# A fused attention and two FFN layers on one core: the first phase issued in the order of its source

## The chip, the cores and the metric

The kernel runs on one core of a Trainium2 chip. The core has a matrix engine (TensorE, PE in the rows), a vector engine (VectorE, DVE), a scalar engine (ScalarE, ACT), GpSimd (POOL) and a queue that issues DMAs (SyncE, SP). Each engine works off its own list of instructions in order; semaphores join the lists. The metric is the time of one execution on the device in microseconds; the kernel before is given by three such runs and by one further execution under the hardware profiler.

## The reference

Attention over 4 batches, 8 heads, 768 positions and 64 features with a local window of 96 and 8 global columns, then two FFN layers of 3072 tokens, 512 wide, 2048 hidden. The FFN weights arrive as 64-bit floats.

```python
scores = scale * np.matmul(q, k.transpose(0, 1, 3, 2))
is_global = pos[None, :] < int(n_global)
is_local = (rel >= 0) & (rel < int(n_local))
scores = scores + bias[None, :, :, :]
scores = np.where(is_global | is_local, scores, -1000000000.0)
a = np.exp(scores - np.max(scores, axis=-1, keepdims=True))
a = a / (np.sum(a, axis=-1, keepdims=True) + 1e-09)
x = np.matmul(a, v)          # then to [tokens, 512]
h = x @ w_in;  x = (h - np.tanh(h)) @ w_out      # first layer
h = x @ w_in2; x = (h * np.cos(h)) @ w_out2      # second layer
```

## The kernel before

**Passes.** Each FFN layer's 16 hidden slices of 128 are cut in two halves of NH = 8, so there are four passes P = 0 to 3. Pass 0 (first half of the first layer) runs during the attention, in blocks of N1 = 256 tokens; passes 1 to 3 follow in blocks of 512 tokens. A block step is ("in", P, j, f): twelve matmuls into h (`ffn_in`), then tanh on ScalarE, a subtraction t and a cast g on VectorE and a remainder on GpSimd; or ("out", P, j, f): twelve matmuls from g into the accumulators c (`ffn_out`). An out step comes two steps of f after its in step. Matmuls run with every operand split into a rounded part and its remainder, three products a matmul.

**Units.** The attention has 24 tiles of 128 tokens and two groups of four heads: 48 units, n = 0 to 47, with tile i = n // 2 and group g = n % 2. Block j of pass 0 needs x of tiles 2j and 2j + 1, so it may begin when unit 4j + 3 is through. A unit has these pieces:
- `load_qk`, `load_v`: DMAs on SP. `qk_T`: four transpositions of q and k into PSUM (tp). `qk_hi` (ScalarE) and `qk_lo` (VectorE) copy them out, split.
- `att_s`: twelve score matmuls into s; then for each of four heads a reduction on VectorE (mask, row extreme, e) and an exponential on ScalarE. After the change the second half is `att_e`, in two parts z = 0, 1.
- `att_n`: sums, reciprocals and four scalings of e on VectorE. `att_t`, z = 0, 1: transpositions of e into tp (one PSUM buffer, shared with `qk_T` outside the early units) and the copy pt on ScalarE.
- `att_v`: matmuls with v into x; then for g = 1 the copies xt, the rounded part on ScalarE and the remainder on VectorE. After the change these copies are `att_x`.

Units are pipelined: in `quad(n)` stand the scores of unit n, the transpositions of unit n - 1 and the values of unit n - 2, with four calls of `ffn_step` between them. The first units (`early_quad`, 0 to 3) have no FFN; `busy` puts idle matmuls there.

**Weights.** Each 128 x 512 weight slice is loaded raw (512 KB) and passes four stages, `w_stage(0..3)`: split (ScalarE copy and GpSimd subtraction), join (two VectorE passes), scale and tail (one ScalarE pass each). `w_step` does all four. Pass 0 needs 16 slices at the start; `w_load_far` puts raw slices in the room of later weights, the rest goes through two raw buffers.

**Order.** A scheduler sets each engine's list when the kernel is built. The kernel before pins part of it: `in_turn` issues a piece after the last matmul of the piece before, and `later` issues weight stages after a marked activation and vector instruction. What is not pinned goes where the scheduler puts it.

## Time and profile before

| what | value |
|---|---|
| median of 3 runs | 1312.69 us (1308.87 to 1313.41) |
| profiled execution, its own time | 1309.77 us |
| its span, first to last instruction | 1308.0 us |
| TensorE busy | 1257.8 us, 96% |
| VectorE busy | 777.2 us, 59% |
| ScalarE busy | 567.8 us, 43% |
| GpSimd busy | 389.8 us, 30% |
| mean granted TensorE clock | 0.986 of full |

Busy shares are averages over stretches of different kinds: the first 100 us hold the early units and the turning of 16 weights, up to 480 us attention and pass 0 run together, the rest is passes 1 to 3. Stretches are therefore read apart. The span leaves out 1.8 us of the execution's own time.

### The profile page before, as it was taken

The page shows a single profiled execution, that of the slowest core. Times are in us where ns is not written, and L with a number is a line of the kernel's source. Part 1 is how long each engine was busy: PE and PEld are TensorE (multiplying, and loading weights), DVE is VectorE, ACT ScalarE, POOL GpSimd, SP SyncE. Part 2 cuts the span into 40 slices and gives each one's busy share as a digit, 9 for nine tenths or more (in the row PEclk, how much of TensorE's full clock was granted, in tenths as well). Part 3 has the DMA queues.
Part 4 walks back from the last instruction along what each step waited for, and adds up shares of the span by engine and source line. Part 5 has one row for each costly group of instructions (what it writes and reads, how often), then busy time and mean ns, then how long its engine had stood idle before and what let it go on. Part 6 is the DMA issues. An engine that isn't in the chain of part 4 may idle for free.

```text
span 1308.0 us, 20613 instructions
## 1 busy us (share of the span) xinstructions
PE 1257.8 (96%) x7616; PEld 1074.2 (82%) x7618; DVE 777.2 (59%) x1813; ACT 567.8 (43%) x1287; POOL 389.8 (30%) x343
## 2 busy tenths in 40 slices
PE   7689999999999999999999999999999999999997
PEld 4578988999998998888888888888888888888885
DVE  7786666667676642344433457777765466555563
ACT  6765555565655531223322334554343333333331
POOL 1341221222222223445544533333332122222221
PEclk9689999999999999999999999999999999999999
DMA  9243334433343343344634432333211312332110
GB/s 274 82 126 100 106 109 124 121 100 95 110 130 108 101 156 104 122 152 161 209 124 153 174 129 81 124 102 127 83 57 72 129 65 68 126 111 83 65 65 35
DMA packets 160845, 149.28 MB, mean 114 GB/s; under 512 B 84960, under 2 KB 119776, under 8 KB 160736
## 3 DMA queue, kind: packets, MB, share of 16 engines
q1 hardware_dynamic: 160448, 147.88, 35.8%
q8 instruction: 62, 1.02, 0.3%
q14 instruction: 47, 0.39, 0.1%
q10 hardware_dynamic: 288, 0.00, 0.0%
HBM read 103.81 MB, written 44.04 MB: 113 GB/s over the span
## 4 chain that ended last, share of the span: by engine, by line
PE 90%; DVE 5%; ACT 3%; issue 1%; DMA 0%; POOL 0%; DVEq 0%; POOLq 0%; ACTq 0%; SPq 0%
PE h L429 41%; PE o L466 20%; PE o L460 10%; PE c L460 10%; PE tp L364 3%; PE s L326 3%; PE x L381 2%; ACT e L342 1%; DVE e L339 1%; PE tp L284 1%; PE tp L286 1%; DVE xt L393 1%; DVE wf L70 1%; DVE e L354 1%; DVE wf L67 0%
## 5 line engine op out<-in xcount | busy, mean ns | idle before, releaser
L445 POOL TENSOR_TENSOR g<-t,g 128x512 fp32r<-128x512 f32 (+1 forms) x240 | 267.7, 1116 | 733.5 <-DVE g L444 647.1
L429 PE MATMUL h<-x,wi 128*128 128x512 f32 x1728 | 423.4, 394 | 0.0
L429 PEld LDWEIGHTS h<-x,wi 128*128 128x128 f32 x1728 | 324.1, 188 | 75.9
L466 PE MATMUL o<-wo,g 128*128 128x512 f32 x1152 | 275.5, 390 | 0.0
L466 PEld LDWEIGHTS o<-wo,g 128*128 128x128 f32 x1152 | 216.3, 188 | 47.1
L429 PE MATMUL h<-xt,wi 128*128 128x256 f32 x1152 | 168.0, 294 | 14.8 <-ACT xt L392 11.1
L438 ACT ACTIVATE t<-h 128x256 f32<-128x256 f32 (+1 forms) x144 | 65.2, 454 | 263.6 <-PE h L429 259.3
L439 DVE TENSOR_TENSOR t<-h,t 128x256 f32<-128x256 f32 (+1 forms) x144 | 73.4, 510 | 171.4 <-ACT t L438 170.5
L429 PEld LDWEIGHTS h<-xt,wi 128*128 128x128 f32 x1152 | 147.4, 194 | 25.3 <-ACT xt L392 13.7
L460 PE MATMUL c<-g,wo 128*128 128x256 f32 x1152 | 161.4, 289 | 0.0
L460 PEld LDWEIGHTS c<-g,wo 128*128 128x128 f32 x1152 | 145.2, 192 | 0.2
L414 ACT ACTIVATE t<-t 128x512 f32<-128x512 f32 x96 | 60.6, 631 | 191.9 <-DVE t L413 191.7
L460 PE MATMUL o<-g,wo 128*128 128x512 f32 x576 | 139.1, 390 | 0.0
L460 PEld LDWEIGHTS o<-g,wo 128*128 128x128 f32 x576 | 108.1, 188 | 23.8
L416 DVE SCALAR_TENSOR_TENSOR t<-t,h 128x512 f32<-128x512 f32 x96 | 65.8, 686 | 101.8 <-ACT t L415 101.6
L342 ACT ACTIVATE e<-e,nmall 128x256 f32<-128x256 f32 (+1 forms) x192 | 92.6, 487 | 76.2 <-DVE nmall L339 76.2
L444 DVE CAST g<-t 128x512 fp32r<-128x512 f32 (+1 forms) x240 | 100.8, 421 | 26.2 <-DMA yd<-g 9.2
L339 DVE CUSTOM_DVE_ANT_0 e<-s,M 128x256 f32<-128x256 f32 (+1 forms) x192 | 69.1, 397 | 68.3 <-PE tp L364 57.6
L411 DVE SCALAR_TENSOR_TENSOR t<-ki,h 128x512 f32<-128x512 int32 x96 | 65.7, 685 | 68.5 <-ACT ki L410 68.3
L410 ACT ACTIVATE ki<-h 128x512 int32<-128x512 f32 x96 | 56.9, 595 | 108.9 <-PE h L429 108.6
L412 DVE SCALAR_TENSOR_TENSOR t<-ki,t 128x512 f32<-128x512 int32 x96 | 87.2, 908 | 2.8
L80 POOL TENSOR_TENSOR wi<-wf,wi 128x512 fp32r<-128x512 f32 x32 | 43.6, 1362 | 92.3 <-ACT wi L79 82.3
(83 smaller groups left out, 1176.8 us busy)
## 6 DMA issues: line engine op xcount, KB each, us to landing
x<-yd SPq DMA_DIRECT2D x48, 512.0 KB, 5.7
raw<-in_moe_w_out_dram SPq DMA_DIRECT2D x28, 512.0 KB, 3.6
raw<-in_moe_w_in_dram SPq DMA_DIRECT2D x27, 512.0 KB, 3.8
xd<-xt SPq DMA_DIRECT2D x12, 1024.0 KB, 5.2
x<-xd SPq DMA_DIRECT2D x24, 512.0 KB, 6.3
yd<-g SPq DMA_DIRECT2D x24, 512.0 KB, 4.0
qn<-in_q_dram SPq DMA_DIRECT2D x48, 128.0 KB, 2.4
kn<-in_k_dram SPq DMA_DIRECT2D x48, 128.0 KB, 2.8
```

The costliest lines, as they stand in the source:

```text
L339: mark[1] = nc.vector.tensor_tensor_reduce(out=e[:, j, 0:n], in0=s[j][:, z, 0:n], in1=M[:, z, m0:m0 + n], scale=slopes[4 * g + j] / base, ...
L342: mark[0] = nc.scalar.activation(out=e[:, j, 0:n], in_=e[:, j, 0:n], func=AF.Exp, scale=-1.0, bias=nmall[:, col:col + 1], accum_out=sm[:, ...
L411: mark[1] = nc.vector.scalar_tensor_tensor(out=r, in0=ki, scalar=-C1, in1=h, op0=ALU.mult, op1=ALU.add)
L412: nc.vector.scalar_tensor_tensor(out=r, in0=ki, scalar=-C2, in1=r, op0=ALU.mult, op1=ALU.add)
L416: nc.vector.scalar_tensor_tensor(out=r, in0=r, scalar=-0.5, in1=h, op0=ALU.add, op1=ALU.mult)
L429: m = nc.tensor.matmul(h, lhsT=wk[:, a], rhs=x[:, b], start=(n == 0), stop=(n == 3 * KC - 1))
L438: mark[0] = nc.scalar.activation(out=t, in_=h, func=AF.Tanh)
L439: mark[1] = nc.vector.tensor_tensor(out=t, in0=h, in1=t, op=ALU.subtract)
L444: nc.vector.tensor_copy(out=g[:, 0], in_=t)
L445: nc.gpsimd.tensor_tensor(out=g[:, 1], in0=t, in1=g[:, 0].bitcast(F32), op=ALU.subtract)
L460: m = nc.tensor.matmul(o[z], lhsT=w[:, a, z * 128:(z + 1) * 128], rhs=g[:, b], start=(f == 0 and n == 0 and (P > 0 or z % 2 == 0)), stop=( ...
L466: nc.tensor.matmul(o[z], lhsT=g[:, a, z * 128:(z + 1) * 128], rhs=w[:, b], start=(f == 0 and n == 0), stop=(last and n == 2))
```

## The change

`in_turn` and `later` go. From the first load to the end of attention (`whole`), `in_order` makes every instruction of an engine follow the one before it in the source, on all five engines, so the order of the source is the order of the lists. The source of that phase is rewritten: score matmuls of the early units stand one unit ahead, in a second PSUM buffer (`att_s(*at(n + 1), ...)` in `early_quad(n)`), there are five early units instead of four, `e` of early units lives in the weight pool, weight stages are written one by one between the pieces (`w_stage`, `w_more`), three far loads are asked for per early unit until the 16 slices are asked for, idle matmuls are 5 + 5 x 8 instead of 9 + 4 x 6, and six empty block steps become two. In the first two steps of a block, the out step of the block before stands ahead of the in step, and where x completes a block (`n % 4 == 1`) `att_x` stands ahead of the exponentials.

```diff
+@contextmanager
+def in_order(tc):
+
+    block = tc.nc.cur_bb
+    done = block.bb.instructions
+    first = done[-1] if done else None
+    yield
+    assert tc.nc.cur_bb is block
+    n = next((k for k in reversed(range(len(done))) if done[k] is first), -1) + 1
+    last = {}
+    for i in done[n:]:
+        if i.engine in last:
+            tc.add_manual_dep(
+                i, last[i.engine].name,
+                mybir.DependencyInfo(mybir.DependencyClass.NoSync, mybir.DependencyReason.DATA), reason="in_order")
+        last[i.engine] = i
+
...
+        Sb[i, g] = (s, sm, n, m0)
+
+    Eb = {}
+
+    def att_e(i, g, z, pool=None):
+
+        s, sm, n, m0 = Sb[i, g]
+        if pool is None:
             e = pa.tile([128, 2, 256], F32, tag="e", name="e", bufs=3)
...
+        else:
+            e = pool.tile([128, 2, 256], F32, tag=("wi", "wo")[z], name="e", bufs=16)
+        for j in range(2):
+            col = i * H + 4 * g + 2 * z + j
+            nc.vector.tensor_tensor_reduce(
+                out=e[:, j, 0:n], in0=s[j][:, z, 0:n], in1=M[:, z, m0:m0 + n], scale=slopes[4 * g + j] / base,
+                scalar=BIG, op0=ALU.add, op1=ALU.min, accum_out=nmall[:, col:col + 1])
+            nc.scalar.activation(
+                out=e[:, j, 0:n], in_=e[:, j, 0:n], func=AF.Exp, scale=-1.0,
+                bias=nmall[:, col:col + 1], accum_out=sm[:, 2 * z + j:2 * z + j + 1])
+        Eb[i, g, z] = e
...
+    def att_x(i, g):
+
+        b, t = where(i)
+        x = Xb[i]
         if g == 1:
...
+    strict = [True]
+    whole = ExitStack()
+    whole.enter_context(in_order(tc))
+    nc.vector.memset(zero, 0.0)
     load_qk(0, 0)
     load_qk(0, 1)
-    nc.vector.memset(zero, 0.0)
...
-    busy(9)
-    with in_turn():
-        qk_T(0, 0)
+    busy(5)
+    qk_T(0, 0)
+    qk_T(0, 1, ps_c, "c0")
     qk_hi(0, 0)
     qk_lo(0, 0)
+    qk_hi(0, 1)
     setup_bias()
-    with in_turn():
-        qk_T(0, 1, ps_c, "c0")
-    qk_hi(0, 1)
-    qk_lo(0, 1)
+    att_s(0, 0)
...
-    def next_qk(n, pool=None, tag="tp"):
+    def next_T(n, pool=None, tag="tp"):
 
         i, g = at(n)
         if i + 1 < NTILE:
             qk_T(i + 1, g, pool, tag)
+        if i + 2 < NTILE:
+            load_qk(i + 2, g)
+        if g == 1 and 0 < i < NTILE - 1:
+            load_v(i + 1)
+
+    def next_qk(n):
+        i, g = at(n)
+        if i + 1 < NTILE:
             qk_hi(i + 1, g)
             qk_lo(i + 1, g)
-        if i + 2 < NTILE:
...
     def early_quad(n):
 
         cur, old, old2 = at(n), at(n - 1), at(n - 2)
-        if old in Sb:
+        for z in range(2):
+            att_e(*cur, z, w_pool)
+        if n == 0:
+            qk_lo(0, 1)
+        if n < 4:
+            att_s(*at(n + 1), None if n % 2 else ps_h)
+        next_T(n, ps_c, "c0")
+        busy(4)
+        if old:
             att_n(*old)
-        with in_turn():
-            att_s(*cur, ps_h if n % 2 else None)
+            att_t(*old, 0)
+        w_stage(1)
+        next_qk(n)
         if n == 0:
-            with later():
-                setup_before()
-        with in_turn():
-            busy(3)
-        with in_turn():
-            next_qk(n, ps_c, "c0")
-        next_v(n)
+            setup_before()
+        if old2:
+            att_v(*old2)
+            att_x(*old2)
         if old:
-            with in_turn():
-                att_t(*old, 0)
-            with in_turn():
-                att_t(*old, 1)
-        with in_turn():
-            busy(3)
-        if old2:
-            with in_turn():
-                att_v(*old2)
-        with later():
-            for _ in range((0, 1, 1, 2)[n]):
-                w_step()
-        for _ in range(2):
-            w_load_far()
+            att_t(*old, 1)
+        busy(4)
+        w_stage(0)
+        w_stage(2)
+        w_stage(3)
+        for _ in range(3):
+            if nload[0] < 2 * NH:
+                w_load_far()
...
         if old in Sb:
             att_n(*old)
         if cur:
-            with in_turn():
-                att_s(*cur)
+            att_s(*cur)
         if old2:
-            with in_turn():
-                att_v(*old2)
+            att_v(*old2)
+        if old2 and n % 4 == 1:
+            att_x(*old2)
+        if cur:
+            att_e(*cur, 0)
+        if old2 and n % 4 != 1:
+            att_x(*old2)
         ffn_step()
         if old:
-            with in_turn():
-                att_t(*old, 0)
+            att_t(*old, 0)
+        if cur:
+            att_e(*cur, 1)
+        w_more(0, 1)
         ffn_step()
         if old:
-            with in_turn():
-                att_t(*old, 1)
+            att_t(*old, 1)
+        if cur:
+            att_n(*cur)
+        w_more(2, 3, 0, 1)
         ffn_step()
         if cur:
-            with in_turn():
-                next_qk(n)
-            next_v(n)
+            next_T(n)
+            next_qk(n)
+        w_more(2, 3, 0, 1)
         ffn_step()
-        if cur:
-            att_n(*cur)
-
-    seq = [None] * 6
+        w_more(2, 3)
+        if n == 5:
+            w_more(0, 1, 2, 3)
+
+    seq = [None]
     for P in range(4):
         steps = [(P, j, f) for j in range(NB[P]) for f in range(NH)]
         done = 0
         for n in range(len(steps) + LAG[P]):
-            if n < len(steps):
-                seq.append(("in",) + steps[n])
-
+
+
+            due = []
             while done < len(steps) and (
                     done <= n - LAG[P] or (P > 0 and done == n - LAG[P] + 1 and steps[done][2] == NH - 1)):
-                seq.append(("out",) + steps[done])
+                due.append(("out",) + steps[done])
                 done += 1
+            now = [("in",) + steps[n]] if n < len(steps) else []
+            if P == 0 and n < 2:
+                seq += now + [None] * (n == 0)
+            elif P == 0 and n % NH < 2:
+                seq += due + now
+            else:
+                seq += now + due
     seq.reverse()
 
-    strict = [True]
-
     def ffn_step():
-        if strict[0]:
-            with in_turn():
-                ffn_part()
-        else:
-            ffn_part()
-
-    def ffn_part():
         step = seq.pop()
         if step is None:
-            with later():
-                w_step()
             return
...
-        if P == 0 and j == 0 and nsplit[0] < 2 * NH:
-            with later():
-                w_step()
-
-        if kind == "out" and P < 3:
-            first = NH if P == 0 else 0
-            share = (j * NH + f - 3 - first) / (NB[P] * NH - 8 - first)
-            n = 4 * (2 * NH + 2)
-            while late.get((P, "stages"), 0) < min(share, 1) * n:
-                late[P, "stages"] = late.get((P, "stages"), 0) + 1
-                with later():
+
+            if P < 3:
+                first = NH if P == 0 else 0
+                late[P] = (j * NH + f - 3 - first) / (NB[P] * NH - 8 - first)
+            if P < 3 and not strict[0]:
+                w_paced(P)
+
+    def w_paced(P):
+        n = 4 * (2 * NH + 2)
+        while late.get((P, "stages"), 0) < min(late.get(P, 0), 1) * n:
+            late[P, "stages"] = late.get((P, "stages"), 0) + 1
+            if strict[0]:
+                w_stage(late[P, "stages"] % 4)
+            else:
+
+                with tc.issue_after(mark[0].ins), tc.issue_after(mark[1].ins):
                     w_stage(late[P, "stages"] % 4)
 
-    for n in range(4):
+    def w_more(*stages):
+
+        if nsplit[0] < 2 * NH:
+            for n in stages:
+                w_stage(n)
+        else:
+            w_paced(0)
+
+    for n in range(5):
         early_quad(n)
-    for n in range(4, len(quads) + 2):
+    for n in range(5, len(quads) + 2):
         if n == 12:
-            with later():
-                flag_n()
+            flag_n()
         quad(n)
     strict[0] = False
+    whole.close()
```

TensorE at the change from block 0 to block 1 (unit 9: s scores, x values, h in step, c out step, tp transpositions), before:

```order
L326 MATMUL s<-kw_96,q_1162 128x256 x12
L381 MATMUL x<-pt,vn 64x128 x8
L429 MATMUL h<-xt,wi 128x256 x12
L364 MATMUL tp<-ident,e 128x128 x4
L460 MATMUL c_1390<-g,wo 128x256 x6
```

and of the change, in the same unit:

```order
L342 MATMUL s<-kw_97,q_1014 128x256 x12
L404 MATMUL x<-pt,vn 64x128 x8
L486 MATMUL c_792<-g,wo 128x256 x6
L486 MATMUL c_793<-g,wo 128x256 x6
L388 MATMUL tp<-ident,e 128x128 x4
L456 MATMUL h<-xt,wi 128x256 x12
```

An out step and four transpositions have moved between the values and the first in step of the new block.

ScalarE in the last early stretch (e exponentials, pt copies of transposed e, raww and wf weight stages, q and kw of `qk_hi`), before, unit 4:

```order
L342 ACTIVATE e,sm<-e,nmall 128x256 x2
L79 ACTIVATE wi<-wf 128x512
L50 ACTIVATE raww<-raww 128x512
L58 ACTIVATE raww<-raww 128x512
L50 ACTIVATE raww<-raww 128x512
L58 ACTIVATE raww<-raww 128x512
L50 ACTIVATE raww<-raww 128x512
L58 ACTIVATE raww<-raww 128x512
L50 ACTIVATE raww<-raww 128x512
L58 ACTIVATE raww<-raww 128x512
L367 ACTIVATE pt<-tp 128x512
```

and of the change, the same unit:

```order
L365 ACTIVATE e,sm<-e,nmall 128x256 x4
L390 ACTIVATE pt<-tp 128x512
L311 ACTIVATE q_548<-tp,qs 128x256
L312 ACTIVATE kw_96<-tp 128x2x128
L390 ACTIVATE pt<-tp 128x512
L97 ACTIVATE wo<-wf 128x512
L68 ACTIVATE raww<-raww 128x512
L76 ACTIVATE raww<-raww 128x512
```

Four weights' scale and tail stood ahead of a copy pt; now both copies of the unit stand ahead of one weight.

VectorE in unit 0 (q and kw of `qk_lo`, tmp and m of `setup_before`), before:

```order
L237 TENSOR_SCALAR tmp<-m,nlng 128x128
L240 COPY m<-m 128x128
L302 SCALAR_TENSOR_TENSOR q_227<-tp,qs,q_227 128x256
L304 TENSOR_TENSOR kw_96<-tp,kw_96 128x2x128
L238 TENSOR_TENSOR m<-m,tmp 128x128
```

and of the change:

```order
L323 CAST kg_99<-kw_97 128x128
L318 SCALAR_TENSOR_TENSOR q_237<-tp,qs,q_237 128x256
L320 TENSOR_TENSOR kw_96<-tp,kw_96 128x2x128
L255 TENSOR_SCALAR tmp<-m,nlng 128x128
L256 TENSOR_TENSOR m<-m,tmp 128x128
```

Before, two rows of `setup_before` stood ahead of `qk_lo` of unit 2; now all of it stands behind.

## Rows read from the trace of the kernel before

**Rows 1.** Windows: busy us (count) of PE, PEld, DVE, ACT, POOL; clock, DMA share, GB/s.

```profile
8.00:46.20 38.20, 21.54 (x155) 14.14 (x157) 28.58 (x107) 27.69 (x79) 4.37 (x4) 0.85 0.79 226
46.20:98.21 52.01, 43.01 (x329) 38.95 (x329) 47.15 (x112) 36.55 (x91) 24.31 (x21) 0.78 0.42 117
98.21:480.00 381.79, 366.87 (x3461) 346.01 (x3461) 251.68 (x884) 216.44 (x627) 84.26 (x98) 1.00 0.38 106
480.00:1308.00 828.00, 819.63 (x3655) 672.20 (x3654) 447.64 (x704) 284.30 (x486) 275.02 (x208) 1.00 0.33 112
```

**Rows 2.** Waits of TensorE, whole span: total us, times, longest.

```profile
PE h L429 <- ACT xt L392: 11.1, 11, 1.4
PE tp L364 <- ACT pt L367: 10.5, 7, 3.6
...
PE h L429 <- DVE xt L393: 3.4, 10, 0.3
```

**Rows 3.** Waits of VectorE, 0 to 100 us: total us, times, longest.

```profile
DVE e L339 <- PE tp L364: 5.0, 3, 3.2
...
DVE wf L67 <- POOL wo L80: 3.2, 1, 3.2
DVE e L339 <- PE s L326: 2.4, 2, 1.7
DVE sm L349 <- ACT e L342: 1.7, 2, 1.0
```

**Rows 4.** Timeline of all engines where block 2 begins.

```profile
137.60 1.09 PE L381 MATMUL x<-pt,vn 128*64 128x128 f32 x16
...
138.83 0.57 ACT L392 ACTIVATE xt<-x 128x512 fp32r<-128x512 f32 x1
139.44 0.69 DVE L393 TENSOR_TENSOR xt<-x,xt 128x512 fp32r<-128x512 f32 x1 [1.21 <-ACT xt L392]
...
139.46 0.38 PE L429 MATMUL h<-xt,wi 128*128 128x256 f32 x1 [0.76 <-ACT xt L392]
...
140.18 1.58 PE L429 MATMUL h<-xt,wi 128*128 128x256 f32 x11 [0.34 <-DVE xt L393]
```

**Rows 5.** Timeline of TensorE in a unit without waits.

```profile
119.25 1.09 PE L381 MATMUL x<-pt,vn 128*64 128x128 f32 x16
120.28 1.70 PE L429 MATMUL h<-xt,wi 128*128 128x256 f32 x12
121.81 0.60 PE L364 MATMUL tp<-ident,e 128*128 128x128 f32 x4
122.17 1.68 PE L460 MATMUL c<-g,wo 128*128 128x256 f32 x12
123.69 0.60 PE L364 MATMUL tp<-ident,e 128*128 128x128 f32 x4
```

**Rows 6.** The page's groups: exponentials and score reductions.

```profile
L342 ACT ACTIVATE e<-e,nmall 128x256 f32<-128x256 f32 (+1 forms) x192 | 92.6, 487 | 76.2 <-DVE nmall L339 76.2
...
L339 DVE CUSTOM_DVE_ANT_0 e<-s,M 128x256 f32<-128x256 f32 (+1 forms) x192 | 69.1, 397 | 68.3 <-PE tp L364 57.6
```

**Rows 7.** Timeline of all engines, end of unit 4.

```profile
40.11 0.65 ACT L50 ACTIVATE raww<-raww 128x512 f32<-128x512 f32 x1
...
43.97 0.65 ACT L58 ACTIVATE raww<-raww 128x512 int32<-128x512 uint16 x1
44.51 0.59 ACT L367 ACTIVATE pt<-tp 128x512 f32<-128x512 f32 x1
...
45.15 0.69 PE L284 MATMUL tp<-ident,qn 128*128 128x128 f32 x2 [5.73 <-ACT pt L367]
```

**Rows 8.** Waits of ScalarE, 0 to 100 us.

```profile
ACT raw L50 <- DMA raw<-in_moe_w_out_dram: 3.6, 1, 3.6
```

**Rows 9.** Timeline of TensorE, idle matmuls.

```profile
8.56 0.82 PE L670 MATMUL idle<-zero 128*128 128x512 bf16 x3
```

**Rows 10.** Timeline of TensorE, an out step in unit 7.

```profile
85.63 2.91 PE L460 MATMUL c<-g,wo 128*128 128x256 f32 x12
```

More of the change, by code (lines that the diff above doesn't have):

```diff
@@ L27, with __init__ @@
 RAWS = 2
+@contextmanager
[13 more added lines that the diff above has]
+        last[i.engine] = i
 class Split:
-    def __init__(self, tc, raw_pool, w_pool):
-        self.nc, self.raw_pool, self.w_pool = tc.nc, raw_pool, w_pool
+    def __init__(self, nc, raw_pool, w_pool):
+        self.nc, self.raw_pool, self.w_pool = nc, raw_pool, w_pool
         self.raw, self.part = {}, {}
@@ L325, in att_s @@
                     r = slice(64 * j, 64 * j + 64)
-                    m = nc.tensor.matmul(s[j][:, z, 0:w], lhsT=a[r, x, z], rhs=kt[r, z, y, 0:w],
-                                         start=(n == 0), stop=(n == 2))
-        piece.append(m)
+                    nc.tensor.matmul(s[j][:, z, 0:w], lhsT=a[r, x, z], rhs=kt[r, z, y, 0:w],
+                                     start=(n == 0), stop=(n == 2))
         if t == 0:
@@ L333, in att_s @@
         sm = pa.tile([128, 8], F32, tag="sm", name="sm", bufs=3)
-        es = []
-        for z in range(2):
-            e = pa.tile([128, 2, 256], F32, tag="e", name="e", bufs=3)
-            for j in range(2):
-                col = i * H + 4 * g + 2 * z + j
-                mark[1] = nc.vector.tensor_tensor_reduce(
-                    out=e[:, j, 0:n], in0=s[j][:, z, 0:n], in1=M[:, z, m0:m0 + n], scale=slopes[4 * g + j] / base,
-                    scalar=BIG, op0=ALU.add, op1=ALU.min, accum_out=nmall[:, col:col + 1])
-                mark[0] = nc.scalar.activation(
-                    out=e[:, j, 0:n], in_=e[:, j, 0:n], func=AF.Exp, scale=-1.0, bias=nmall[:, col:col + 1], accum_out=sm[:, 2 * z + j:2 * z + j + 1])
-            es.append(e)
-        Sb[i, g] = (es, sm, n)
+        Sb[i, g] = (s, sm, n, m0)
[3 more added lines that the diff above has]
+        if pool is None:
+            e = pa.tile([128, 2, 256], F32, tag="e", name="e", bufs=3)
+        else:
[9 more added lines that the diff above has]
+        Eb[i, g, z] = e
     def att_n(i, g):
-        es, sm, n = Sb.pop((i, g))
+        s, sm, n, m0 = Sb.pop((i, g))
+        es = [Eb.pop((i, g, z)) for z in range(2)]
         nc.vector.tensor_scalar(out=sm[:, 0:4], in0=sm[:, 0:4], scalar1=1e-9, scalar2=None, op0=ALU.add)
@@ L380, in att_v @@
                 for j in range(2):
-                    m = nc.tensor.matmul(x[64 * j:64 * j + 64, p], lhsT=vv[:, 2 * p + j], rhs=pt[:, 2 * c + j],
-                                         start=(c == 0), stop=(c == nch - 1))
-        piece.append(m)
+                    nc.tensor.matmul(x[64 * j:64 * j + 64, p], lhsT=vv[:, 2 * p + j], rhs=pt[:, 2 * c + j],
+                                     start=(c == 0), stop=(c == nch - 1))
+    def att_x(i, g):
+        b, t = where(i)
+        x = Xb[i]
         if g == 1:
@@ L428, in ffn_in @@
             for a, b in ((0, 0), (0, 1), (1, 0)):
-                m = nc.tensor.matmul(h, lhsT=wk[:, a], rhs=x[:, b], start=(n == 0), stop=(n == 3 * KC - 1))
+                nc.tensor.matmul(h, lhsT=wk[:, a], rhs=x[:, b], start=(n == 0), stop=(n == 3 * KC - 1))
                 n += 1
-        piece.append(m)
         if P == 0:
@@ L459, in ffn_out @@
                 if P < 2:
-                    m = nc.tensor.matmul(o[z], lhsT=w[:, a, z * 128:(z + 1) * 128], rhs=g[:, b],
-                                         start=(f == 0 and n == 0 and (P > 0 or z % 2 == 0)), stop=(last and n == 2),
-                                         skip_group_check=(P == 0))
-                    if z == 3 and n == 2:
-                        piece.append(m)
+                    nc.tensor.matmul(o[z], lhsT=w[:, a, z * 128:(z + 1) * 128], rhs=g[:, b],
+                                     start=(f == 0 and n == 0 and (P > 0 or z % 2 == 0)), stop=(last and n == 2),
+                                     skip_group_check=(P == 0))
                 else:
@@ L596, in general_ffn @@
             ps = g.enter_context(tc.tile_pool(name="gps2", bufs=1, space=PSUM))
-            gs = Split(tc, rp, None)
+            gs = Split(nc, rp, None)
             wf = {}
@@ L669, in busy @@
         for _ in range(n):
-            m = nc.tensor.matmul(idle, lhsT=zero[:, 0:128], rhs=zero, start=True, stop=True)
-        piece.append(m)
-    @contextmanager
-    def in_turn():
-        with tc.issue_after(piece[-1].ins):
-            yield
+            nc.tensor.matmul(idle, lhsT=zero[:, 0:128], rhs=zero, start=True, stop=True)
+    strict = [True]
+    whole = ExitStack()
+    whole.enter_context(in_order(tc))
+    nc.vector.memset(zero, 0.0)
     load_qk(0, 0)
     load_qk(0, 1)
-    nc.vector.memset(zero, 0.0)
     setup()
```

18 lines of the change are left out of this document (3 added, 15 removed).

## The prediction

> **What bounds the kernel now.** I read the busy times by stretch first. Four stretches are cut at places in the program: 8 us (first scores), 46.2 us (scores of unit 5), 98.2 us (scores of unit 9), 480 us (attention done) [rows 1]. From 480 us on TensorE is busy 819.6 of 828 us, and the change does not reach there. From 98.2 to 480 us it is busy 366.9 of 381.8 us at full clock: 14.9 us idle. Before 98.2 us it is idle 16.7 + 9.0 us and its granted clock is 0.85 and 0.78 of full, so there something else sets the pace. In 46.2 to 98.2 us that is VectorE, busy 47.2 of 52.0 us; ScalarE has 36.6. In 8 to 46.2 us no engine is full (TensorE 21.5, VectorE 28.6, ScalarE 27.7 of 38.2): they wait for each other.
>
> Second, who TensorE waits for [rows 2]. Eleven waits of the first h matmul of a token block on ScalarE's half of xt (11.1 us), and ten right behind them on VectorE's half (3.4 us): 14.5 us, one pair for each of the blocks 1 to 11, all at or after 98.2 us. That is nearly all of TensorE's idle time there. Of the rest, all early, 10.5 us are waits of the transpositions of e on the copy pt.
>
> Third, who VectorE waits for in the first 100 us [rows 3]: TensorE's transpositions 5.0 us, a weight's subtraction on GpSimd 3.2, scores 2.4, the exponentials 1.7.
>
> **The change part by part, with its price.** No arithmetic is added or taken away except idle matmuls, so the sum is made of waits.
>
> *Block order and x (term B).* Before, h of a new block stands directly behind the last x matmuls. In block 2 [rows 4] x starts at 137.60; the same 16 matmuls elsewhere take 1.03 us from start to next start (119.25 to 120.28, [rows 5]), so TensorE was free at 138.63. ScalarE's half ran from 138.83, VectorE's ended at 140.13, and the other eleven h matmuls went on at 140.18: x is complete 1.55 us after TensorE could use it. After the change an out step (122.17 to 123.69, 1.52 us) and four transpositions (121.81 to 122.17, 0.36 us) [rows 5] stand between: 1.88 us of work, 0.33 us more than x needs, and in those units ScalarE's half is put ahead of the exponentials. So the whole 14.5 us should go. Given back: the exponentials of that unit start only behind VectorE's half. Two score reductions (about 0.4 us each) and two exponentials (about 0.5 each) [rows 6] overlap as a chain of about 1.5 us from 140.13, to 141.6; the copy pt (0.59, [rows 7]) ends at 142.2. TensorE, having done out, transpositions and the h step (1.53) after 138.63, asks for pt's PSUM tile at 142.04. That is 0.2 us, eleven times: 2 us; short units (128 columns) need less. I take 1.5. **B = -14.5 + 1.5 = -13**, from -14.5 (no wait) to -10 (0.4 us lost a block).
>
> *Early units: scores one ahead, weights spread, order of the source (term A).* The work of VectorE up to unit 9's scores is the same: 17 weights are joined in both kernels (5 and 12 in the two stretches before; 4 and 13 after, as the order shows). So the most that can be won is VectorE's idle time in the two stretches, 9.6 + 4.9 = **14.5 us** [rows 1]. I go through what made it:
> - A burst. In unit 4 ScalarE has eight weight passes in a row, 40.11 to 44.5 us, with the copy pt behind them; TensorE waits 5.73 us for that copy [rows 7], and VectorE ends up waiting 3.2 us for a weight behind it [rows 3]. After the change one weight per early unit is scaled, split and joined, behind both copies. Gone: 3.2, and 3.2 to 4 of the 5.0 us on transpositions.
> - Scores. Waits of 2.4 us for s: scores stand a unit ahead and wait in a second PSUM buffer. Gone: about 1.7 (0.7 is at 99 us).
> - Exponentials, 1.7 us: the sums used are now those of the unit before, whose exponentials are done. Gone.
> - New: in unit 0 VectorE's row after the reductions is qk_lo of unit 2, which waits for ScalarE's qk_hi behind four exponentials, and setup_before is queued behind it, where it filled the gap before. I put 2 us there, from the four exponentials (0.49 each, [rows 6]).
> Sum: 3.2 + 3.6 + 1.7 + 1.7 - 2 = 8.2, and the weight loads, now all asked for in the early units, no longer come two at a time through the two raw buffers; one landing late held ScalarE for 3.6 us [rows 8], partly under VectorE's work, so 1 us of it. **A = -9**, from 0 (in-order queues put new waits in place of the old) to -14.5 (VectorE full).
>
> *Idle matmuls (term C).* busy() issues 45 matmuls instead of 33. Three take 0.82 us [rows 9], so 12 more are 3.3 us. They stand in early units, where TensorE has 16.7 us of slack and waits for copies; cost 0, and +3.3 if the cover were gone.
>
> *Queue of loads.* SP now issues three weight loads per early unit instead of two, ahead of later q and k loads. Those are asked for two units before use, some 12 us; cost 0, and a late one costs a few us once, within A's range.
>
> *ffn_step without work.* Six None steps become two, with one early unit more: at unit 9 both kernels have issued 14 block steps, and 14 are left after the attention. No gain by itself.
>
> Sum: -9 - 13 = **-22 us**. The profiled execution took 1309.77 us (its span was 1308.0); 1309.8 - 22 = 1287.8. The median of the three timed runs is 1312.7, 2.9 us above the profiled one, so I forecast **1289 us**. A measurement of this kernel can tell about 0.5% (6.5 us) from no change.
>
> One row speaks against A. In 46.2 to 98.2 us the granted clock averages 0.78 [rows 1], and an out step that takes 1.68 us at full clock [rows 5] took 2.91 us there [rows 10]: part of the stretch runs at the 1.2 instead of the 2.4 GHz level, after a stretch in which TensorE had waited 5.73 us at one place. The Trainium skill, TensorE: Matmul & The Clock Gate, section "HAM oscillation — how this bites in real kernels", says the same of kernels whose matmul bursts alternate with waits: after each such wait the burst starts cold again. By that rule units 5 to 8, in which TensorE still waits for VectorE, would run slow throughout, and the sum would be that of rival 3. By the row, 0.78 is full clock for (0.78 - 0.5) / 0.5 = 56% of the stretch, although VectorE set its pace; with shorter waits I take full clock for as much or more.
>
> **The rivals.**
> 1. *Early stretch not shorter.* ScalarE and VectorE now run a fixed order in which each waits for the other once a unit. For it: VectorE is already 91% busy from 46.2 us on, and qk_lo and join wait for ScalarE's rows. Against: the burst is gone. A = 0 to -4: 1309.8 - 13 - 2 = 1295, with the medians' offset 1296.
> 2. *VectorE full.* A = -14.5, B = -14.5: 1281, with the offset 1282.
> 3. *The clock stays at half in units 5 to 8.* A full unit is 366.87 / 41 = 8.95 us of TensorE work [rows 1]; at half clock a step takes 2.91 instead of 1.68 us [rows 5, 10], 1.73 times, so 15.5 us; four units 62 us instead of 52. Then A = -6 (what is won up to unit 5) + 10 = +4, total -9: 1301, or up to 1308 if early units lose too.
> 4. *Slower: the exponentials of the second half stand in every unit behind the FFN's subtraction and cast.* On VectorE the second two reductions come after the subtraction of the first h step. That step ends 3.5 us into a unit; tanh, subtraction and cast put the reductions at 4.6, the exponentials end at 6.1, the second copy pt at 6.7, and TensorE asks for its PSUM tile at 7.3. The margin is 0.6 us. If GpSimd's work stretches VectorE's casts beyond it, TensorE waits in each of the 41 units; it decides from 0.7 us a unit (22 + 6.5 over 41). At 1 us: 1309.8 - 22 + 41 = 1329. Against it: before, TensorE waited for nothing but xt in these units with nearly the same rows [rows 2].
>
> **How the numbers follow.** Forecast (1283 to 1295) 0.58; rival 1 0.17; rival 2 0.11; rival 3 0.08, half of it within 0.5%; rival 4 0.06. Faster by over 0.5%: 0.58 + 0.17 + 0.11 + 0.04 = 0.90; within 0.5%: 0.04; slower: 0.06. The range 1279 to 1302 takes in B's and A's bounds and the better half of rival 3, and leaves out about 0.12.
>
> **What would show it.** B: no wait of h on xt at blocks 1 to 11, and TensorE idle under 4 us from unit 9's scores to the end of attention; wrong if a wait on pt of over 0.4 us stands in every fourth unit. A: scores of unit 9 at 86 to 92 us instead of 98.2, those of unit 5 at 36 to 40 instead of 46.2, no wait on raw. The forecast is wrong upwards if unit 9 still starts near 98 us (rival 1, or 3 if the clock there is near 0.5), and downwards if it starts before 85.

## The result and the profile after

The changed kernel takes 1296.1 us (median of four runs, 1295.4 to 1296.7), the kernel before, run in turn with it, 1313.1 us: a ratio of 0.9875, with a 95% interval of 0.9851 to 0.9899. The forecast was 1289 us, in a range of 1279 to 1302. The profiled executions took 1309.8 us before and 1296.1 us after (spans 1308.0 and 1294.3), so 13.7 us are to be found in the traces, where the prediction's sum had 22.

The windows of the changed kernel, cut at its own scores of units 5, 9 and 10, answer to [rows 1]:

```profile
8.00:38.20 30.20, 24.74 (x171) 15.59 (x174) 26.07 (x108) 22.96 (x73) 3.88 (x3) 1.00 1.09 321
38.20:90.84 52.64, 39.95 (x330) 36.54 (x329) 47.15 (x109) 38.42 (x95) 22.28 (x19) 0.90 0.30 85
90.84:104.48 13.64, 10.96 (x89) 10.13 (x88) 11.24 (x28) 7.14 (x19) 3.86 (x4) 0.87 0.49 153
104.48:480.00 375.52, 370.88 (x3485) 350.25 (x3485) 249.82 (x876) 219.43 (x622) 84.07 (x102) 1.00 0.41 114
480.00:1294.30 814.30, 806.22 (x3544) 658.78 (x3542) 442.41 (x692) 281.20 (x477) 270.96 (x203) 1.00 0.32 109
```

Unit 5 starts 8.0 us earlier (38.20 for 46.20), unit 9 7.4 us earlier (90.84 for 98.21). But unit 9 itself now takes 13.64 us instead of 10.96 (before, it ran from 98.21 to 109.17), so unit 10 starts only 4.7 us earlier. Units 5 to 8 take as long as they did, with VectorE busy for the same 47.15 us. The other 9 us come in the rest of the attention: the last x matmuls start at 463.14 instead of 475.28, the next pass at 488.85 instead of 502.25.

TensorE's waits over the whole span of the changed kernel answer to [rows 2]:

```profile
PE tp L388 <- ACT pt L390: 13.9, 10, 4.8
PE tp L301 <- ACT pt L390: 3.8, 10, 1.1
PE s L342 <- DVE q L318: 2.7, 1, 2.7
PE h L456 <- DVE xt L420: 2.6, 2, 2.3
```

The eleven waits of h on ScalarE's half of xt are gone, and of those on VectorE's half one counts, 2.3 us at block 1. Waits on the copy pt are about as long in all, 17.7 us (13.9 and 3.8); before, they were 18.7 us, the 10.5 us of [rows 2] and this row of the same view:

```profile
PE tp L284 <- ACT pt L367: 8.2, 3, 5.7
```

What is new is where they stand. Those after unit 9 alone (104 to 520 us) are these:

```profile
PE tp L301 <- ACT pt L390: 2.7, 9, 0.5
PE tp L388 <- ACT pt L390: 1.8, 2, 1.0
```

So in the steady part 13.0 us of waits on xt went and 4.5 us on pt came; before, TensorE waited for no pt at all there. Five of these eleven waits, 0.2 us each and 1.1 in all, stand in units in which a block begins; 3.4 us stand in units 15, 19, 30 and 39, where none does.

**Why unit 9 is long.** The timeline of the changed kernel in unit 9, with rows of VectorE, two of GpSimd's, and TensorE's scores and h:

```profile
90.13 1.87 POOL L98 TENSOR_TENSOR wo<-wf,wo 128x512 fp32r<-128x512 f32 x1 [0.83 <-ACT wo L97]
...
90.84 0.98 PE L342 MATMUL s<-kw,q 64*128 64x256 f32 x12
90.87 1.67 DVE L88 SCALAR_TENSOR_TENSOR wf<-raww,wf 128x512 int32<-128x512 int32 x1
...
92.46 0.41 DVE L465 TENSOR_TENSOR t<-h,t 128x256 f32<-128x256 f32 x1
...
94.11 1.28 POOL L98 TENSOR_TENSOR wo<-wf,wo 128x512 fp32r<-128x512 f32 x1
94.15 1.78 DVE L85 SCALAR_TENSOR_TENSOR wf<-raw 128x512 int32<-128x512 int32 x1
...
95.97 0.69 DVE L88 SCALAR_TENSOR_TENSOR wf<-raw,wf 128x512 int32<-128x512 int32 x1
96.58 0.69 DVE L420 TENSOR_TENSOR xt<-x,xt 128x512 fp32r<-128x512 f32 x1
...
97.18 0.42 DVE L362 CUSTOM_DVE_ANT_0 e<-s,M 128x256 f32<-128x256 f32 x1
...
97.32 1.57 PE L456 MATMUL h<-xt,wi 128*128 128x256 f32 x11 [2.29 <-DVE xt L420]
```

TensorE computes the scores at 90.84. VectorE gets to them at 97.18, 5.4 us after they are there: three instructions that join weights still stand ahead, q and k of unit 10, and xt of block 1. TensorE had run ahead of the engine that sets the pace. The wait is not all of the 2.7 us by which unit 9 is longer: TensorE is idle for 2.7 us in it (1.5 before) and busy for 10.96 (9.51 before). Its out step at 92.77 takes 1.70 us; the one at 100.04, behind the wait, takes 2.65, at the 1.2 GHz level, and the unit's granted clock is 0.87 (1.00 before). In the kernel before VectorE reached unit 9 without a backlog; its row, and the window from 8 us to that row:

```profile
99.23 0.43 DVE L339 CUSTOM_DVE_ANT_0 e<-s,M 128x256 f32<-128x256 f32 x1 [0.75 <-PE s L326]
```

```profile
8.00:99.23 91.23, 65.56 (x496) 53.98 (x500) 76.00 (x219) 64.25 (x170) 29.10 (x24) 0.81 0.58 163
```

And the same stretch of the changed kernel:

```profile
8.00:97.18 89.18, 68.87 (x544) 55.81 (x547) 79.38 (x226) 63.74 (x170) 29.29 (x24) 0.94 0.56 161
```

With 17 weights joined in both, VectorE reaches unit 9 at 97.18 instead of 99.23: **2.05 us** earlier, not 7.4. Its idle time fell from 15.2 (91.23 - 76.00) to 9.8 us, but its work rose by 3.4 us. The joins took 1.9 us longer; 0.7 is xt of block 1, which stood behind this row before (at 101.30); about 1.1 is set-up that VectorE had done ahead of 8 us before (busy 2.15 us there, now 1.03); other rows took less. Counted with xt behind the row in both, VectorE is 2.7 us early.

### The profile page after: what moved, and what is told of

It reads as the page before. It is cut to its first block, busy times and chain, and to the rows that moved or that the text cites. A ratio compares the mean times of both kernels' runs of the same rounds, so it can differ in the third digit from the quotient of the medians.

```text
span 1294.3 us, 20600 instructions
## 1 busy us (share of the span) xinstructions
PE 1258.1 (97%) x7627; PEld 1073.5 (83%) x7630; DVE 777.7 (60%) x1813; ACT 571.9 (44%) x1287; POOL 387.0 (30%) x343
## 4 chain that ended last, share of the span: by engine, by line
PE 87%; DVE 6%; ACT 5%; issue 1%; DMA 1%; SPq 0%; DVEq 0%; ACTq 0%
PE h L456 39%; PE o L490 20%; PE o L486 10%; PE c L486 8%; PE x L404 3%; PE s L342 3%; ACT e L365 2%; PE tp L388 2%; DVE wf L85 1%; PE tp L301 1%; DVE e L362 1%; DVE wf L88 1%; DVE e L378 1%; ACT pt L390 1%; PE tp L303 1%
## 5 line engine op out<-in xcount | busy, mean ns | idle before, releaser
L471 POOL TENSOR_TENSOR g<-t,g 128x512 fp32r<-128x512 f32 (+1 forms) x240 | 263.9, 1100 | 767.0 <-DVE g L470 677.8
L456 PE MATMUL h<-xt,wi 128*128 128x256 f32 x1152 | 165.2, 294 | 2.7 <-DVE xt L420 2.6
L470 DVE CAST g<-t 128x512 fp32r<-128x512 f32 (+1 forms) x240 | 95.2, 397 | 26.4 <-DMA yd<-g 5.2
L388 PE MATMUL tp<-ident,e 128*128 128x128 f32 x352 | 57.0, 282 | 15.6 <-ACT pt L390 13.9
```

Of the source, the lines that this page charges most:

```text
L388: nc.tensor.transpose(tp[:, 2 * c + j], e[:, j, c * 128:(c + 1) * 128], ident)
L456: nc.tensor.matmul(h, lhsT=wk[:, a], rhs=x[:, b], start=(n == 0), stop=(n == 3 * KC - 1))
L470: nc.vector.tensor_copy(out=g[:, 0], in_=t)
L471: nc.gpsimd.tensor_tensor(out=g[:, 1], in0=t, in1=g[:, 0].bitcast(F32), op=ALU.subtract)
```

## The experiments

Theory 1, formed from the two traces, has both terms in it: the block order takes the waits on xt away (term B); the early units gain little because VectorE is nearly full up to unit 9 (term A); and the waits on pt come from the fixed order on VectorE, where score reductions stand behind FFN work. The main rival is that the gain comes from the early units and the fixed order as such.

Each kernel was timed in five rounds in turn with the kernel before. "VectorE at unit 9" is the start of its first score reduction there, "next pass" the start of the first h after the attention, both from the profiled execution.

| kernel | us | ratio to before (95%) | VectorE at unit 9 | next pass |
|---|---|---|---|---|
| before | 1309.8 to 1313.1 | 1 | 99.23 | 502.25 |
| changed | 1296.1 | 0.9875 (0.9851 to 0.9899) | 97.18 | 488.85 |
| no_b | 1324.2 | 1.0120 (1.0104 to 1.0135) | 98.12 | 516.41 |
| no_swap | 1309.7 | 0.9997 (0.9988 to 1.0006) | 97.82 | 501.84 |
| x_late | 1301.9 | 0.9942 (0.9929 to 0.9956) | 98.43 | 493.77 |
| before_swap | 1292.5 | 0.9869 (0.9854 to 0.9884) | 99.82 | 484.56 |
| red_first | 1292.4 | 0.9860 (0.9841 to 0.9879) | 97.77 | 484.09 |
| join_one | 1282.2 | 0.9783 (0.9767 to 0.9799) | 87.31 | 474.20 |
| scores_late | 1296.5 | 0.9887 (0.9868 to 0.9906) | 98.49 | 490.21 |
| weights_lump | 1303.4 | 0.9941 (0.9926 to 0.9955) | 106.39 | 496.54 |
| no_busy | 1297.1 | 0.9897 (0.9882 to 0.9912) | 99.59 | 491.04 |
| red_kg | 1290.3 | 0.9846 (0.9832 to 0.9859) | 96.26 | 483.71 |
| red_kg_setup | 1290.8 | 0.9852 (0.9838 to 0.9865) | 95.87 | 483.54 |
| red_kg_setup_hold | 1287.7 | 0.9828 (0.9814 to 0.9841) | 93.93 | 480.15 |

### Which part carries the gain

**no_swap**: the changed kernel with the order of out and in undone.

```diff
             elif P == 0 and n % NH < 2:
-                seq += due + now
+                seq += now + due
```

> The changed kernel with only the order of out and in at a block's start undone; the copy of x stays ahead of the exponentials in those units. Theory 1: TensorE is free 1.3 to 1.55 us before x is complete, as before the change, so eleven waits on xt and +8 to +13 us, 1304 to 1309 us, and less than with both halves undone, since here ScalarE's half of xt is not behind exponentials. Rival (the place of x ahead of the exponentials is what counts): 1296 to 1299 us.

Measured 1309.7 us, a ratio of 0.9997: all of the gain is gone, a little more than theory 1 gave (1304 to 1309). The waits of TensorE from 104 to 520 us show waits on xt again, 9.9 us (13.0 in the kernel before), and 2.9 of the 4.5 us on pt beside them:

```profile
PE h L456 <- ACT xt L419: 6.7, 10, 0.7
PE h L456 <- DVE xt L420: 3.2, 9, 0.4
PE tp L301 <- ACT pt L390: 1.7, 4, 0.5
PE tp L388 <- ACT pt L390: 1.2, 2, 1.0
```

**before_swap**: the kernel before with that one edit alone.

```diff
+            late_in = P == 0 and n >= 2 and n % NH < 2
-            if n < len(steps):
+            if n < len(steps) and not late_in:
                 seq.append(("in",) + steps[n])
             while done < len(steps) and (
...
+            if n < len(steps) and late_in:
+                seq.append(("in",) + steps[n])
```

> The kernel before with one part of the change alone: out ahead of in at the first two steps of blocks 1 to 11. Theory 1: 14.5 us of waits on xt fall away, some 2 to 5 us come back on pt: -9 to -13 us against the kernel before, 1300 to 1304 us. Rival (the gain comes from the early units and the fixed order): 1311 to 1314 us.

Measured 1292.5 us against 1309.8, 17.3 us less: more than expected, and no slower than the whole change. Where block 2 begins, against [rows 4], x is complete at 138.93 and TensorE, busy with an out step and two transpositions until 139.10, goes on with h without a wait:

```profile
136.40 1.09 PE L381 MATMUL x<-pt,vn 128*64 128x128 f32 x16
137.43 1.70 PE L460 MATMUL c<-g,wo 128*128 128x256 f32 x12
...
137.63 0.57 ACT L392 ACTIVATE xt<-x 128x512 fp32r<-128x512 f32 x1
138.24 0.69 DVE L393 TENSOR_TENSOR xt<-x,xt 128x512 fp32r<-128x512 f32 x1 [1.22 <-ACT xt L392]
...
139.10 1.68 PE L429 MATMUL h<-xt,wi 128*128 128x256 f32 x12
```

From 104 to 520 us TensorE waits only 0.5 us for anything:

```profile
PE tp L284 <- ACT pt L367: 0.5, 2, 0.3
```

Both waits stand in units where a block begins. So the 3.4 us of waits on pt elsewhere do not belong to the block order but to the order that the rest of the change fixed.

The waits on xt make 14.5 of the 17.3 us. Nearly all of the rest is in h itself. A step that its wait on VectorE's half cuts in two takes 0.38 + 1.58 us [rows 4], an uncut one 1.70 [rows 5]: 0.26 us more in each of eleven blocks, 2.9 us. The busy time of h in pass 0 falls by as much, from 168.0 us before to 165.1 us here (165.2 in the changed kernel).

**x_late**: only the place of x is undone.

```diff
-        if old2 and n % 4 == 1:
-            att_x(*old2)
         if cur:
             att_e(*cur, 0)
-        if old2 and n % 4 != 1:
+        if old2:
             att_x(*old2)
```

> The changed kernel with only the place of x undone: in every unit the copy of x stands behind the first two reductions and exponentials (about 1.5 us). Theory 1: the out step and the transpositions cover 1.88 us and x needed 1.55 us, a margin of 0.33 us, so some 1 us of wait at each of eleven blocks, less the waits on pt that fall away: +4 to +11 us, 1300 to 1307 us. Rival (the order of out and in alone does all of B): 1294 to 1297 us.

1301.9 us, inside what theory 1 gave; the span is 5.8 us longer than the changed kernel's. Only 1.4 us of that arise between unit 10's scores and the last x (360.05 for 358.66 us), where waits on xt of 3.0 us stand against 1.2 us less on pt; 3.5 us are lost before unit 10 (its scores at 108.02 for 104.48), where VectorE reaches unit 9 1.3 us later; no run tells where the rest of that comes from. The margin of 0.33 us was thus nearly enough in the steady part.

**no_b**: the edits of no_swap and x_late together.

> The changed kernel with both halves of term B undone: at the start of a token block the step h stands again directly behind the x matmuls, and the copy of x always stands behind the first two exponentials. Theory 1 (B and A each carry a part): a wait of h on xt comes back at blocks 1 to 11, 1.3 us or more each, against 4.5 us of waits on pt that the change put there; so +9 to +20 us over the changed kernel, 1305 to 1316 us. Rival (the gain is all from the early units and from the fixed order): 1296 to 1298 us.

1324.2 us: 28 us above the changed kernel and 14 above the kernel before, more than either theory gave. In a fixed order, h behind x and x behind two exponentials, the waits on xt reach 17.0 us (14.3 and 2.7; the longest 2.9 instead of 1.4). What the place of x costs depends on the block order: 14.6 us with h behind x (no_swap to no_b), 5.8 us with out between.

### Where the waits on pt come from

The timeline of the changed kernel in unit 15, rows of VectorE, ScalarE and TensorE:

```profile
152.71 0.58 ACT L419 ACTIVATE xt<-x 128x512 fp32r<-128x512 f32 x1
...
153.32 0.69 DVE L420 TENSOR_TENSOR xt<-x,xt 128x512 fp32r<-128x512 f32 x1 [1.30 <-ACT xt L419]
...
153.93 0.42 DVE L465 TENSOR_TENSOR t<-h,t 128x256 f32<-128x256 f32 x1
...
154.38 0.29 DVE L470 CAST g<-t 128x256 fp32r<-128x256 f32 x1
...
154.59 0.42 DVE L362 CUSTOM_DVE_ANT_0 e<-s,M 128x256 f32<-128x256 f32 x1
...
155.56 0.50 ACT L365 ACTIVATE e<-e,nmall 128x256 f32<-128x256 f32 x1
...
156.05 0.58 ACT L390 ACTIVATE pt<-tp 128x512 f32<-128x512 f32 x1
...
156.68 0.44 PE L301 MATMUL tp<-ident,qn 128*128 128x128 f32 x2 [0.49 <-ACT pt L390]
```

The second two reductions stand behind xt, subtraction and cast on VectorE; ScalarE's exponentials wait for them, with the copy pt queued behind. This is the prediction's rival 4 in small: 0.49 us here, and in four units instead of 41.

**red_first** puts the two reductions ahead of the step (att_e is cut into its reductions, part 1, and its exponentials, part 2; ScalarE's order stays).

```diff
...
+        if cur:
+            att_e(*cur, 1, part=1)
         ffn_step()
         if old:
             att_t(*old, 0)
         if cur:
-            att_e(*cur, 1)
+            att_e(*cur, 1, part=2)
```

> The changed kernel with one edit from unit 5 on: VectorE's two score reductions of the second half stand ahead of the subtraction and cast of the unit's first FFN step; ScalarE's order is untouched. Theory 1 (the 4.5 us of waits on pt after unit 9 come from reductions queued behind FFN work on VectorE, which makes the exponentials in front of the second copy pt late): those waits fall under 1.5 us, the time to 1291 to 1293.5 us. Rival (pt is late through ScalarE's own order): waits on pt stay at 4 us or more, 1295 to 1298 us.

1292.4 us, as theory 1 said. No execution of it (1291.6 to 1293.3) reaches into the changed kernel's range, but the two were timed in different rounds and the intervals of their ratios overlap. The traces bear the gain out: from unit 10's scores to the next pass it takes 380.4 us for 384.4, and the waits on pt after unit 9 fall from 4.5 to 2.0 us (theory 1: under 1.5). The same unit in this kernel:

```profile
151.74 0.69 DVE L424 TENSOR_TENSOR xt<-x,xt 128x512 fp32r<-128x512 f32 x1 [1.30 <-ACT xt L423]
...
152.34 0.41 DVE L365 CUSTOM_DVE_ANT_0 e<-s,M 128x256 f32<-128x256 f32 x1
...
153.03 0.42 DVE L469 TENSOR_TENSOR t<-h,t 128x256 f32<-128x256 f32 x1
...
153.86 0.60 ACT L394 ACTIVATE pt<-tp 128x512 f32<-128x512 f32 x1
...
155.04 0.38 PE L301 MATMUL tp<-ident,qn 128*128 128x128 f32 x2
```

pt now ends at 154.46, 0.58 us before TensorE comes to its tile; the waits in units 15 and 19 are gone. What is left is 1.0 us in the units where a block begins, 0.7 in unit 30 and 0.3 in unit 39.

**red_kg** is red_first with one more edit: the copy of the global keys (L326), now `kg_in`, moves behind the first two reductions.

```diff
...
         if cur:
             att_e(*cur, 0)
+        if n > 5 and at(n - 1) and at(n - 1)[0] + 1 < NTILE:
+            i, g = at(n - 1)
+            kg_in(i + 1, g)
```

> The kernel with the reductions first, and one more edit from unit 6 on: the copy of the global keys (0.33 us) moves from the end of the unit before to behind the first two reductions. Theory 1 (what is left of the waits on pt is VectorE being late at a unit's start): the 2.0 us of waits on pt fall under 1 us, 1290.5 to 1292 us. Rival (that row is on no chain that ends at a copy pt): 1292 to 1293.5 us.

1290.3 us; but pt waits are 1.8 us, not under 1, and the next pass starts 0.4 us earlier than in red_first. Theory 1's number for the waits failed, and the 2 us between the medians are not separated from chance (the intervals of the ratios overlap, and so nearly do the executions, 1289.0 to 1291.5 for 1291.6 to 1293.3). Nothing is shown for this edit.

### What the early units gain from

**join_one**: VectorE's work is made less. It leaves out the second of the two instructions that join a weight, so the weights lose their sign.

```diff
-        nc.vector.scalar_tensor_tensor(
-            out=a, in0=t[:, :, 1], scalar=-0x80000000, in1=a, op0=ALU.bitwise_and, op1=ALU.bitwise_or
-        )
```

> The changed kernel with the second of the two VectorE instructions that join a weight's words left out (the weights lose their sign): 17 instructions of about 0.9 us, 15 us, less on VectorE up to unit 9's first score reduction. Theory 1 (VectorE sets the pace there): that reduction moves from 97.2 to between 84 and 89 us, and the time falls by 8 to 13 us, to 1283 to 1288 us. Rival (ScalarE and the fixed order set the pace): the reduction stands after 93 us, 1292 to 1296 us.

1282.2 us, and VectorE at unit 9 at 87.31: 9.9 us earlier, of 15 taken out. VectorE sets the pace there. It does not do so alone: with the work gone, it waits for ScalarE more, up to that row 6.7 us for qk_hi (3.0 in the changed kernel) and 3.5 for tanh (2.7). From 8 to 100 us, 12.7 us past that row:

```profile
DVE t L462 <- ACT t L461: 6.8, 5, 1.9
DVE q L315 <- ACT kw L309: 6.7, 5, 2.8
```

**scores_late**: att_s of units 0 to 4 back at the start of their own unit.

```diff
-    att_s(0, 0)
...
+        att_s(*cur, ps_h if n % 2 else None)
         for z in range(2):
             att_e(*cur, z, w_pool)
...
-        if n < 4:
-            att_s(*at(n + 1), None if n % 2 else ps_h)
```

> The changed kernel with the scores of units 0 to 4 back at the start of their own unit. Theory 1 (scores ahead were worth about 2 us of VectorE's idle time): unit 9's first score reduction moves by +2 to +4 us, 1298 to 1300 us. Rival (the wait is absorbed before unit 9, because weights joined meanwhile need not be joined later): within 1 us of the changed kernel, 1295 to 1297 us.

1296.5 us, the changed kernel's 1296.1 within its spread: for the time the rival holds. VectorE waits 1.8 us for s again and reaches unit 9 1.3 us later, so little of the wait is absorbed before unit 9; in the time it cannot be seen.

**weights_lump**: the weights of units 0 to 4 are turned at the end of each unit.

```diff
-        w_stage(1)
         next_qk(n)
...
-        w_stage(0)
-        w_stage(2)
-        w_stage(3)
+        for _ in range((0, 1, 1, 2, 2)[n]):
+            w_step()
```

> The changed kernel with the early weights turned in a lump at the end of each unit, 0, 1, 1, 2 and 2 of them. Theory 1 (the burst of weight passes ahead of the copies pt was worth 3 us or more): TensorE and VectorE wait in units 3 to 5 again, unit 9's first score reduction moves by +2 to +5 us, 1298 to 1301 us. Rival (VectorE's total of work sets unit 9, and five weights instead of four are joined before unit 5): within 1 us, 1295 to 1297 us.

1303.4 us, 7.3 us above the changed kernel, more than expected; VectorE at unit 9 is 9.2 us later, though five weights instead of four are joined before VectorE's first reduction of unit 5. In a fixed order a lump stands ahead of the copies of the next unit; VectorE waits 9.5 us for qk_hi (3.0 in the changed kernel):

```profile
DVE q L318 <- ACT kw L312: 9.5, 5, 2.8
```

**no_busy**: the idle matmuls of units 0 to 4 are left out.

```diff
         next_T(n, ps_c, "c0")
-        busy(4)
...
             att_t(*old, 1)
-        busy(4)
```

> The changed kernel without the 40 idle matmuls of units 0 to 4 (the five at the very start stay). Theory 1 (they lie in TensorE's slack, the prediction's term C of 0): unit 9's first score reduction stays within 1 us of 97.2 us, 1295 to 1297 us. Rival 1 (they are on the path): it comes 3 us earlier, 1292 to 1293.5 us. Rival 2 (they hold the granted clock): the clock in 8 to 38 us falls from 1.00 towards 0.7 and units 1 to 9 are late by 3 to 10 us, 1299 to 1306 us.

1297.1 us, 1 us above, as theory 1 said of the time. In the profiled execution VectorE at unit 9 comes at 99.59, 2.4 us later, where it said within 1 us: the direction of rival 2, under its price. But that execution, 1298.6 us, is the slowest of its four, and the intervals of the ratios overlap; a loss of time is not shown. The granted clock of no_busy in units 3 and 4:

```profile
30.00:36.00 6.00, 3.43 (x20) 2.13 (x18) 5.41 (x19) 5.37 (x16) 1.28 (x1) 0.75 1.05 299
36.00:38.80 2.80, 2.69 (x20) 2.17 (x20) 2.35 (x6) 2.28 (x8) 0.00 (x0) 0.57 1.07 367
```

In the changed kernel it is 1.00 throughout that stretch ([rows 1] had 0.85 up to 46.2 us). So they are not idle in effect: they hold the 2.4 GHz level. What that is worth is at most some 2 us.

### Towards a better kernel

**red_kg_setup**: in unit 0 setup_before goes ahead of next_qk on VectorE, the place where the prediction had put 2 us.

```diff
         w_stage(1)
-        next_qk(n)
         if n == 0:
             setup_before()
+        next_qk(n)
```

> As the kernel with both reductions and key copy moved, and in unit 0 the second half of the bias set-up stands ahead of qk_lo of unit 2 on VectorE instead of behind it. Theory 1 (VectorE sets the pace from unit 1 to unit 9, and there it waits 2.8 us at this place): unit 1's first reduction moves from 17.6 to about 15.7 us and unit 9's by 1.5 to 2 us; 1289 to 1290.5 us. Rival (the gain is used up by ScalarE before unit 9): unit 9's moves by less than 0.7 us, no change of time.

1290.8 us, no change. VectorE starts unit 1 1.5 us earlier (16.26 for 17.79), unit 2 0.4 us earlier, unit 9 0.4 us earlier: the rival holds, the gain is used up within one unit.

**red_kg_setup_hold**: the seventeenth weight, needed only in the next pass, is joined after unit 9.

```diff
             for n in stages:
-                w_stage(n)
+                if n != 1 or nsplit[0] < 2 * NH:
+                    w_stage(n)
```

> As the kernel before it, and the seventeenth weight, the first of the next pass, is joined after unit 9 instead of ahead of VectorE's half of xt for block 1. Theory 1 (the longer unit 9 is VectorE's backlog): the 2.3 us wait of the first h of block 1 on xt goes, and with it 2 to 2.5 us; 1286.5 to 1288.5 us. Rival (the backlog is given back at the exponentials of unit 9 or by the later join): within 1 us of the kernel before it.

1287.7 us, 3.1 us less than without this edit (1286.4 to 1288.4 against 1290.2 to 1291.1). xt of block 1 no longer stands behind a join; VectorE and TensorE in unit 9:

```profile
93.33 0.68 DVE L427 TENSOR_TENSOR xt<-x,xt 128x512 fp32r<-128x512 f32 x1
...
93.93 0.42 DVE L368 CUSTOM_DVE_ANT_0 e<-s,M 128x256 f32<-128x256 f32 x1
...
94.17 1.68 PE L463 MATMUL h<-xt,wi 128*128 128x256 f32 x12
```

It is the best of the kernels that compute the reference, 0.9828 of the kernel before.

## Why the prediction was right, and where not

The sign and the range held. The time, 1296.1 us, lies 7 us above the forecast, just outside the 1283 to 1295 that had the chance of 0.58, and on the 1296 of rival 1. Term B came out near its size, in part because two errors in its sum cancel; term A was mis-sized by 7 us and a price of the fixed order was missing. That the range held all this was partly luck.

**Term B, forecast -13.** Its mechanism was right: out and transpositions cover x. The swap is worth -13.6 us inside the change (no_swap to changed, 1309.7 to 1296.1). The sum behind the forecast was not quite this one. One wait on xt stayed, that of block 1 (2.3 us), because of VectorE's backlog in unit 9 and not of the exponentials. The give-back was put at 0.2 us in eleven units, 1.5 us in all, and is 0.2 us in five, 1.1 us. And the 0.26 us by which a wait lengthens an h step were left out: 2.8 us (168.0 to 165.2). By these rows it is -14.5 + 2.6 + 1.1 - 2.8 = -13.6. Nor is the size B's own: in the order of the kernel before, the swap alone gives -17.3 us, and in the new order swap and place of x together are worth -28.1 (no_b to changed). The terms do not add up as the prediction had them.

Its sign for B, TensorE idle under 4 us from unit 9's scores to the end of attention, failed: it is idle 2.7 us in unit 9 and 4.6 from there to 480 us.

**Term A, forecast -9.** The step that failed is its measure and its sum. I took "the most that can be won" as VectorE's idle time up to unit 9's scores, its work being the same. The idle time fell by 5.4 us, but the work up to that row rose by 3.4 us, of which the joins are 1.9 (17 weights took 28.5 us to join before and 30.4 after, the sum of their rows) and the rest is mostly rows that changed places. That leaves 2.05 us. "Scores of unit 9 at 86 to 92 us" came true (90.84), and so did unit 5's, and both proved nothing: TensorE's scores can run ahead of VectorE's backlog. Of the pieces, spreading the weights is worth 7.3 us in this fixed order; the scores a unit ahead are worth nothing that can be measured. The 2 us put down for unit 0 are in the trace, a wait of 2.8 us for qk_hi, but taking 1.5 of them away moved unit 9 by 0.4 us (red_kg_setup).

**The missing term.** Writing all of it in a fixed order has a price: 3.4 us of waits on pt after unit 9 outside the block starts, and a join ahead of xt in unit 9. Together with A it comes to nothing: without the swap the rest of the change is 0.9997 of before. How this nothing is made up of A's gain and the order's price stays open, since no run has the early units or the fixed order alone. red_first takes 3.7 us back (1296.1 to 1292.4), the held join 3.1.

**Term C and the queue of loads, 0.** For loads the trace bears it out: no wait on raw is left, and TensorE's longest wait for q or k is 0.9 us. For term C the medians agree with 0 (1297.1 without 40 of the idle matmuls, 1296.1 with them).

**The rivals.** Rival 1 gave 1296 us, and its mechanism (ScalarE and VectorE in a fixed order wait for each other; early gain 0 to 4 us) is the better account of the early units. Rival 2 fell with VectorE's 9.8 us of idle time. Rival 3 fell: the granted clock in units 5 to 8 rose from 0.78 to 0.90, although TensorE waits 12.4 us on pt between 38 and 104 us. But the clock does fall behind the long ones of these waits, as in unit 8, where the out step before the wait had taken 1.68 us:

```profile
85.65 1.12 PE L388 MATMUL tp<-ident,e 128*128 128x128 f32 x4 [2.75 <-ACT pt L390]
86.41 2.63 PE L456 MATMUL h<-xt,wi 128*128 128x256 f32 x12
...
89.24 1.67 PE L486 MATMUL c<-g,wo 128*128 128x256 f32 x12
```

Behind the waits of 4.78 and 2.96 us in units 6 and 7 the next step took 2.91 and 2.85 us, the one after it 1.68 and 1.67. The Trainium skill, TensorE: Matmul & The Clock Gate, section "HAM oscillation — how this bites in real kernels", says that a burst of matmuls behind such a wait starts cold, and the trace agrees. That units 5 to 8 would therefore run slow throughout was a step beyond the page, and the measured 0.90 decides against it. Rival 4 named the right rows on VectorE, but its 0.6 us of margin mostly held: waits of 0.5 to 1.6 us in four units, not 1 us in 41.

## What to carry to other kernels

Mark progress on the engine that sets the pace, not on TensorE: count how much of that engine's queued work is done when a stage begins, or an early start of the stage will look like a gain. When several edits come as one change, put the edit with the clearest wait to remove alone into the old kernel; here one edit gave as much as the whole rewrite. A hand-written order has to be read queue by queue for what stands ahead of the row that another engine waits for, and work that nobody needs yet belongs behind it.

## What the runs showed of the hardware

A join instruction on VectorE takes 0.69 us (95.97 above), but 1.67 at 90.87 and 1.78 at 94.15. The first started while a GpSimd subtraction ran (90.13 to 92.00), the second 0.04 us after another (94.11 to 95.39), and each ended 0.54 us after the subtraction did. The Trainium skill, SBUF — State Buffer, section "SBUF: two separate sides", says that a VectorE instruction with two SBUF inputs, as these are, and a GpSimd one that reads SBUF share a port pair, and whoever starts second waits for the whole of the other; these rows agree. So does every join instruction over 0.75 us up to unit 9, 7 of 34 in the kernel before, 10 in the changed one, 8 in no_swap: each started during a GpSimd subtraction and ended 0.54 or 0.55 us after it. So the joins' time goes by where GpSimd's subtractions fall, which is how the same 17 weights came to 28.5, 30.4 and, in no_swap, 28.4 us.

The idle matmuls were worth 0.75 against 1.00 of granted clock in units 3 and 4, and little or nothing in time, since VectorE, and not TensorE, was the engine that was late.
